# One PSUM bank per copy of transposed Q and K, and a new order of the work

## The chip, the core and the metric

The kernel runs on one core of one Trainium2 chip. The core has five engines with queues of their own: TensorE (PE in the profile; its weight loads are PEld), VectorE (DVE), ScalarE (ACT), GpSimd (POOL) and SyncE (SP), which here only issues transfers. Transfers between main memory and the core's SBUF run on 16 DMA engines. Matmul results land in PSUM, which has eight banks; here the whole of PSUM is one tile, `bank`, and the program names the bank of every step. The metric is device time in microseconds (us), median of the runs.

## The reference

For 8 batches and 8 heads, sequence 576, head size 64: causal attention with a decay, then a gated layer with a causal convolution of five taps.

```
scores = q @ k.T / 8
cum    = cumsum(max(s, 0))
scores = where(causal future, -1e9, scores + min(-(cum_i - cum_j), 0))
attn   = exp(scores - max) ; attn /= sum(attn)
x      = attn @ v                                # heads side by side: [8, 576, 512]
gate   = sigmoid(sum over k of conv_w[k] * x shifted by 4 - k)
out    = (gate * (x @ w_val)) @ w_out            # float32 [8, 576, 512]
```

The data are drawn once; q, k and v are float32 and are rounded to bfloat16 in the kernel.

## The kernel before, in words

The heads are worked in pairs: pair n = 4b + p holds heads 2p and 2p + 1 of batch b, 32 pairs in all. The steps of a pair, by the names that the program gives them:

- `ld_q`, `ld_k`, `ld_v`, `ld_t`, `ld_s` (L376 to L470) load. For batch 0, `ld_q.0.p` and `ld_k.0.p` bring the first 512 tokens of one pair. For later batches `ld_k.b` and `ld_q.b` each bring q and k together, `ld_q` for pairs 0 and 1, `ld_k` for pairs 2 and 3, into one of the tiles `first` or `qkf` (a slot number stands in the order). `ld_t` brings the last 64 tokens.
- `c_q`, `c_k` (L440) cast them to bfloat16 (`qkb`); `qt` (batch 0, L499) or `qq` (later batches, L647) transposes them on TensorE into PSUM; `qe` (L505) copies the transposed Q and K from PSUM into `QKT`. `tt` and `te` do the same for the last 64 tokens.
- `s0`, `s1`, `s2`, `s4` are the score matmuls, `e0`, `e1`, `e2`, `e4` the exponentials on ScalarE (L568, L544) and `mk` the causal mask on GpSimd (L591), for those pairs that are not masked by a matmul on TensorE (L530).
- `scan`, `decT`, `expw` make the decay weights from s, `vp` (L473) multiplies V by them on GpSimd, `av0` and `av` (L606) multiply the probabilities with that, `rec` and `nm` normalise, `xt` and `xe` transpose the result.
- `p2` to `p4` and `t1` to `t4` are the convolution on VectorE, GpSimd and ScalarE (L667, L678, L683, L686), `th` the tanh, `val` (L716) and `out` (L736) the two big products, `glu` the gating, `oe` and `st` the copy out and the store.
- `wu` (L632) multiplies the identity into a bank that nobody reads: work that only fills TensorE's time.

For batches 1 to 7 a step `qq.b.h` transposes pairs 2h and 2h + 1 and names two banks. Each pair takes sixteen transposes, eight for each of two token halves: r = 0 are the first 256 tokens, on 64 of the partitions, r = 1 the next 256, on the other 64. The half r goes into the r-th bank named, the first pair into its first 512 columns, the second into its last 512. A `qe.b.p` then copies pair p, and so reads one half of each of the two banks.

The order of all steps is written out in the string `ORDER` (L192), one entry per step: name, engine (S, G, T, A, V for SP, POOL, PE, ACT, DVE), PSUM banks or buffer slots. It comes from a planner. Each engine works off its own entries in that order. Waits between engines follow from the buffers that the steps read and write, and for PSUM from the banks. A transfer also waits until the one that used its completion counter eight transfers earlier has landed.

Of the kernel before, what the change touches and what calls it, by code (L numbers as in the profile page):

```python
# [212 lines left out]
te.2:A t1.4:V:3 av.5:T e1.7:A c_q.2:G:0 ld_v.3.2:S val.3.0:T:1 rec.5:V ld_t.4:S val.3.1:T:4 p4.4:A:0 nm.5:V
val.1.0:T:5 c_k.2:A:1 glu.3.0:V xt.5:T:6 t4.4:G glu.3.1:V ld_q.5:S:3 val.1.1:T:7 xe.5:V s2.7:T:3+4 glu.1.0:V
qq.2.0:T:1:2 t1.5:V:2 p2.5:G:1 e2.7:A val.0.0:T:5 glu.1.1:V glu.0.0:V qe.2.0:A val.0.1:T:7 t2.5:G t2.4:V av0.7:T:4+5
p3.5:A:0 av.7:T glu.0.1:V t3.4:V val.2.0:T:3 qe.2.1:A cast_wo:G qq.2.1:T:6:7 rec.7:V nm.7:V val.2.1:T:2 qe.2.3:A
xt.6:T:1 glu.2.1:V xt.7:T:0 t3.5:G qe.2.2:A glu.2.0:V s0.9:T:4+5:2 xe.6:V out.0.2:T:3 xe.7:V e0.9:A t1.6:V:1 p4.5:G:1
s1.9:T:6+7 t1.7:V:0 out.0.0:T:2 e1.9:A p3.6:G:0 t4.6:V s1.8:T:4+5 oe.0.2:A:0 s0.8:T:6+7:1 t4.7:V t4.5:G oe.0.0:A:1
val.7.0:T:3 e0.8:A t2.6:V st.0.0:S out.0.3:T:2 t2.7:V e1.8:A t3.6:G val.4.0:T:1 out.0.1:T:6 t3.7:V th.4:A:2 c_q.3:G:1
val.7.1:T:7 th.6:A:0 oe.0.3:V:2 val.4.1:T:0 glu.4.0:V th.7:A:1 oe.0.1:V:3 s2.8:T:4+5 s4.2.3:T:1+2 e2.8:A glu.4.1:V  # L220
st.0.1:S val.6.0:T:6 vp.2.0:G ld_v.3.3:S val.6.1:T:0 e4.2.3:A glu.6.0:V st.0.2:S glu.7.1:V s2.9:T:4+5 th.5:A:2
vp.2.1:G s0.10:T:1+2:0 ld_v.3.0:S glu.6.1:V av0.8:T:6+7 glu.7.0:V e2.9:A ld_v.3.1:S av.8:T vp.2.2:G val.5.0:T:3
st.0.3:S e0.10:A rec.8:V ld_q.4:S:1 nm.8:V s2.10:T:4+5 val.5.1:T:0 e2.10:A vp.2.3:G glu.5.0:V s1.10:T:6+7 glu.5.1:V
s0.11:T:1+2:1 ld_v.3.4:S e1.10:A xt.8:T:3 tt.3:T:0 ld_k.5:S:4 mk.10:G xe.8:V av0.9:T:4+5 e0.11:A t1.8:V:2 av.9:T
p4.8:G:0 qq.3.0:T:6:7 te.3:A rec.9:V nm.9:V s1.11:T:1+2 qe.3.0:A out.0.7:T:0 p3.8:G:1 t2.8:V qe.3.1:A av0.10:T:4+5
oe.0.7:V:1 c_k.3:G:1 xt.9:T:3 av.10:T e1.11:A xe.9:V s0.12:T:6+7:0 rec.10:V t1.9:V:0 out.0.6:T:0 e0.12:A mk.11:G
nm.10:V s1.12:T:1+2 oe.0.6:A:0 s2.11:T:6+7 t3.9:V xt.10:T:4 e1.12:A t3.8:G st.0.6:S out.0.8:T:0 ld_k.4:S:2 xe.10:V
e2.11:A t1.10:V:1 s2.12:T:1+2 c_q.5:G:0 tt.4:T:5 ld_v.4.1:S e2.12:A oe.0.8:V:3 qq.3.1:T:6:7 st.0.7:S t4.9:V qe.3.2:A
ld_v.4.0:S av0.11:T:1+2 t2.10:V p3.10:G:1 av.11:T ld_t.5:S qe.3.3:A out.0.4:T:0 rec.11:V t4.10:V t4.8:G te.4:A
st.0.8:S s0.14:T:6+7:1 nm.11:V out.0.5:T:4 e0.14:A oe.0.4:V:2 t3.10:G xt.11:T:5 th.8:A:2 t2.9:V s4.3.3:T:6+7 st.0.4:S  # L230
s0.13:T:0+1:2 ld_v.4.2:S e4.3.3:A xe.11:V mk.14:G s2.13:T:2+3 th.10:A:1 ld_v.4.4:S val.8.0:T:6 t1.11:V:2 val.10.0:T:7
e0.13:A ld_v.4.3:S vp.3.1:G glu.8.0:V t3.11:V ld_k.6:S:3 val.8.1:T:6 e2.13:A s1.13:T:0+1 glu.10.0:V c_q.4:G:1 t2.11:V
th.9:A:0 val.10.1:T:7 val.9.0:T:2 glu.8.1:V e1.13:A glu.10.1:V val.9.1:T:3 t4.11:V c_k.5:G:2 oe.0.5:A:0 s2.14:T:6+7
qq.5.0:T:0:1 e2.14:A glu.9.1:V st.0.5:S av0.13:T:4+5 qe.5.1:V av.13:T qe.5.0:A vp.3.2:G val.11.0:T:3 rec.13:V
glu.9.0:V th.11:A:1 s1.14:T:6+7 s0.15:T:0+1:2 nm.13:V val.11.1:T:2 vp.3.3:G e1.14:A glu.11.0:V xt.13:T:4 glu.11.1:V
e0.15:A s1.15:T:6+7 xe.13:V mk.12:G s2.15:T:2+3 out.1.1:T:5 t1.13:V:2 e1.15:A c_k.4:G:0 t2.13:V qq.5.1:T:0:1 e2.15:A
av0.14:T:6+7 qe.5.3:V av.14:T qe.5.2:A out.1.2:T:2 mk.15:G rec.14:V p4.13:A:1 nm.14:V qq.4.0:T:0:1 oe.1.1:A:3 t4.13:G
qq.4.1:T:6:7 oe.1.2:A:1 qe.4.1:V qe.4.0:A xt.14:T:5 out.1.0:T:2 vp.3.0:G t3.13:V xe.14:A av0.15:T:0+1 oe.1.0:A:2
t1.14:V:0 av.15:T p2.14:G:1 qe.4.2:A ld_v.5.4:S av0.12:T:2+3 rec.15:V ld_v.5.1:S av.12:T nm.15:V qe.4.3:A p4.14:G:0
tt.5:T:4 ld_v.5.2:S rec.12:V t3.14:V xt.15:T:0 te.5:A ld_v.5.0:S s0.16:T:6+7:0 xe.15:A nm.12:V s2.16:T:4+5 ld_v.5.3:S  # L240
vp.4.1:G e0.16:A t1.15:V:1 ld_t.6:S xt.12:T:3 s0.17:T:1+2:2 e2.16:A xe.12:V t2.14:G s4.4.3:T:6+7 t3.15:V ld_q.6:S:2
e0.17:A s1.16:T:4+5 t1.12:V:3 vp.4.0:G e4.4.3:A st.1.0:S t2.15:V val.14.0:T:1 st.1.1:S e1.16:A s1.17:T:6+7 t2.12:V
ld_k.7:S:4 t4.14:G val.14.1:T:2 e1.17:A t4.15:V av0.16:T:4+5 av.16:T ld_q.7:S:1 vp.4.3:G t4.12:V th.14:A:1 s2.17:T:6+7
out.1.3:T:0 rec.16:V e2.17:A t3.12:V st.1.2:S c_k.6:G:0 nm.16:V th.13:A:0 s0.18:T:6+7:0 val.12.0:T:3 e0.18:A
glu.14.1:V val.12.1:T:4 glu.14.0:V vp.4.2:G xt.16:T:2 oe.1.3:V:0 th.12:A:2 s4.5.3:T:6+7 xe.16:V s1.18:T:0+1 e4.5.3:A
glu.12.1:V val.13.0:T:5 mk.18:G e1.18:A glu.12.0:V s2.18:T:6+7 t1.16:V:3 val.13.1:T:3 vp.5.1:G e2.18:A glu.13.0:V
val.15.0:T:4 t4.16:V val.15.1:T:5 th.15:A:2 vp.5.2:G s0.19:T:6+7:1 glu.13.1:V av0.18:T:0+1 e0.19:A glu.15.1:V av.18:T
# [605 lines left out]
```

## Time and profile before

| what | us |
|---|---|
| median of 3 runs | 198.42 (197.47 to 199.06) |
| the profiled execution, its time | 198.85 |
| its span, first to last instruction | 197.0 |
| PE busy | 175.7 (89%) |
| ACT busy | 171.2 (87%) |
| POOL busy | 167.0 (85%) |
| DVE busy | 164.4 (83%) |

Durations in the profile come from the one profiled execution; its time lies 1.85 us above its span and 0.43 us above the median. In the rows, an arrow points from what is read to what is written (`out<-in`), the number after x is the count, and what stands behind "<-" in brackets is what ended the engine's idle time. L373 is the line of the helper that makes every plain copy, so its rows have to be told apart by the tile: `QKT<-bank` is a `qe` (or `te`), `qkb<-first` a cast.

### The profile page before, as it was taken

How to read it: one execution, taken by the hardware profiler on the slowest of the kernel's cores; microseconds unless marked ns; L12 is line 12 of the kernel's file. 1: busy time of each engine (PE TensorE's matmuls, PEld its weight loads, DVE VectorE, ACT ScalarE, POOL GpSimd, SP SyncE). 2: the span in 40 equal slices, each digit the busy share in tenths (PEclk: the TensorE clock that was granted, in tenths of full speed). 3: DMA queues.
4: the chain of work that ended last, by engine and by line, in shares of the span. 5: the costliest groups of instructions: out<-in, count | busy, mean ns of one | idle time of the engine just before them, and what ended most of it. 6: DMA issues, size and time to landing. Idle time of an engine off the chain costs nothing.

```text
span 197.0 us, 6662 instructions
## 1 busy us (share of the span) xinstructions
PE 175.7 (89%) x2716; PEld 115.6 (59%) x2716; DVE 164.4 (83%) x320; ACT 171.2 (87%) x229; POOL 167.0 (85%) x152
## 2 busy tenths in 40 slices
...
GB/s 169 280 202 207 239 259 253 276 254 284 279 145 287 271 323 297 319 339 236 292 88 225 236 405 330 211 204 255 8 208 61 3 0 161 112 3 106 5 174 205
DMA packets 62284, 40.46 MB, mean 205 GB/s; under 512 B 47334, under 2 KB 49382, under 8 KB 62251
## 3 DMA queue, kind: packets, MB, share of 16 engines
...
HBM read 30.57 MB, written 9.44 MB: 203 GB/s over the span
## 4 chain that ended last, share of the span: by engine, by line
PE 55%; ACT 19%; DVE 13%; DMA 6%; issue 3%; POOL 2%; ACTq 0%; DVEq 0%
PE bank L736 14%; ACT P L568 11%; PE bank L606 10%; PE bank L716 10%; PE bank L517 9%; DVE QKT L373 4%; DMA first<-in_q_dram 4%; ACT QKT L373 3%; PE bank L638 3%; DVE gp L683 3%; PE bank L641 3%; ACT th L703 3%; DVE glu L725 2%; PE bank L632 2%; DVE gp L678 2%
## 5 line engine op out<-in xcount | busy, mean ns | idle before, releaser
L568 ACT ACTIVATE P<-bank 128x1024 bf16<-128x1024 f32 x84 | 82.8, 1047 | 7.5 <-PE bank L517 5.1
L686 POOL TENSOR_TENSOR gp<-gp,pr 128x572 f32<-128x572 f32 (+6 forms) x37 | 46.1, 1250 | 7.1 <-DVE gp L683 3.6
L683 DVE SCALAR_TENSOR_TENSOR gp<-bank,cwr,gp 128x573 f32<-128x573 bf16 (+5 forms) x71 | 51.3, 743 | 0.5
L517 PE MATMUL bank<-QKT 64*128 64x128 bf16 (+4 forms) x592 | 39.6, 244 | 7.8 <-ACT P L568 3.5
L473 POOL TENSOR_TENSOR Vp<-vst,w 128x650 bf16<-128x650 f32 x32 | 40.5, 1283 | 0.8 <-ACT w L394 0.8
L716 PE MATMUL bank<-xT,wv 128*128 128x288 bf16 (+2 forms) x256 | 38.3, 286 | 1.1 <-ACT P L568 0.5
L606 PE MATMUL bank<-Vp,P 128*128 128x65 bf16 x960 | 36.4, 196 | 0.9 <-ACT QKT L373 0.4
L606 PEld LDWEIGHTS <-P 128*128 128x128 bf16 x960 | 33.6, 99 | 5.9 <-issue 2.9
L736 PE MATMUL bank<-wo,glu 128*128 128x512 bf16 x144 | 36.3, 380 | 0.0
L517 PEld LDWEIGHTS <-QKT 64*128 64x128 bf16 x592 | 20.4, 96 | 24.5 <-issue 19.7
L667 POOL TENSOR_TENSOR pr<-xT,cwr 128x572 f32<-128x572 bf16 (+6 forms) x28 | 27.5, 994 | 2.4 <-ACT xT L373 1.7
L725 DVE SCALAR_TENSOR_TENSOR glu<-th,bank 128x288 bf16<-128x288 f32 (+2 forms) x64 | 27.3, 446 | 2.3 <-PE bank L716 0.6
L716 PEld LDWEIGHTS <-wv 128*128 128x128 bf16 x256 | 22.6, 97 | 11.0 <-issue 4.8
L678 DVE SCALAR_TENSOR_TENSOR gp<-xT,cwr,bank 128x576 f32<-128x576 bf16 (+2 forms) x36 | 26.4, 741 | 2.0 <-ACT xT L373 1.2
L625 DVE TENSOR_TENSOR xn<-bank,recs 128x640 bf16<-128x640 f32 (+2 forms) x36 | 26.7, 744 | 0.6
L373 ACT COPY QKT<-bank 128x1024 bf16<-128x1024 bf16 (+1 forms) x24 | 23.0, 997 | 4.7 <-DVE QKT L373 2.0
L591 POOL TENSOR_SCALAR_AFFINE_SELECT P<-P 128x1024 bf16<-128x1024 bf16 (+2 forms) x22 | 23.1, 1052 | 4.0 <-ACT P L568 4.0
L703 ACT ACTIVATE th<-gp,cwr 128x576 f32<-128x576 f32 x28 | 21.9, 801 | 0.0
L736 PEld LDWEIGHTS <-glu 128*128 128x128 bf16 x144 | 12.3, 98 | 13.3 <-issue 2.3
L373 POOL CAST qkb<-first 128x512 bf16<-128x512 f32 (+2 forms) x11 | 12.0, 1095 | 7.2 <-DMA first<-in_q_dram 6.7
L373 ACT COPY ot<-bank 128x512 f32<-128x512 f32 x28 | 16.2, 605 | 2.0 <-PE bank L736 1.2
L373 DVE COPY QKT<-bank 128x512 bf16<-128x512 bf16 (+1 forms) x12 | 11.5, 956 | 7.1 <-PE bank L502 4.9
...
## 6 DMA issues: line engine op xcount, KB each, us to landing
out_dram<-ot SPq DMA_DIRECT2D x36, 256.0 KB, 3.2
vst<-in_v_dram SPq DMA_DIRECT2D x28, 256.0 KB, 5.4
...
vst<-in_v_dram SPq DMA_DIRECT2D x15, 128.0 KB, 5.1
first<-in_q_dram SPq DMA_DIRECT2D x6, 256.0 KB, 4.2
```

What stands on the lines that cost most here:

```text
L373: (act.copy if e is act else e.tensor_copy)(dst, src)
L473: e.tensor_tensor(Vps[b % 2][:, :, HP[p]], vslot(b)[:, :, HP[p]], w[:, :, b * 8 + 2 * p:b * 8 + 2 * p + 2].unsqueeze(3).to_broadcast([128, ...
L517: pe.matmul(ps[:, hh, c0:c0 + nq], QKTs[b % 2][r, 1, p, k0:k0 + 128], QKTs[b % 2][r, 0, p, q0:q0 + nq], **kw)
L568: act.activation(out=Pt(n)[:, :, step * 512:(step + 1) * 512], in_=pair((f"s{step}", n)), func=AF.Exp, scale=0.125)
L606: pe.matmul(ps[:, o:o + 65], lhsT, Vps[b % 2][:, kb, 2 * p + w, :], start=(kb == 0), stop=(kb == qb))
L678: vec.scalar_tensor_tensor(gp[:, lo:hi], xT[:, 3 + lo:3 + hi], r, xps(n, *h)[:, lo:hi], ALU.mult, ALU.add)
L683: vec.scalar_tensor_tensor(gp[:, lo:hi], xps(n, *h)[:, lo - m:hi - m], r, gp[:, lo:hi], ALU.mult, ALU.add)
L686: pool.tensor_tensor(gp[:, lo:hi], gp[:, lo:hi], prs[at[f"p{m}", n, *h][0]][:, lo:hi], ALU.add)
L703: act.activation(out=thof(n)[:, r], in_=gps[at["t1", n][0]].rearrange("p (h s) -> p h s", h=2)[:, r], func=AF.Tanh, scale=cwr[:, n % 4, 4:5])
L716: pe.matmul(ps, wv[:, dc, c * 128:(c + 1) * 128], xTs[b % 2][:, dc, 4 + lo:4 + hi], start=(dc == 0), stop=(dc == 3))
L725: vec.scalar_tensor_tensor(glu2[:, c, o + lo:o + hi], th[:, lo:hi], 1.0, ps, ALU.add, ALU.mult)
L736: pe.matmul(bank_of(u, i), glu2[:, c, i * 128:i * 128 + 128], wo[:, c, :], start=(c == 0), stop=(c == 3))
```

## The change

Three things change.

- A step `qe.b.p` of batches 1 to 7 no longer copies pair p. With h = p // 2 and r = p % 2 it copies token half r of both pairs 2h and 2h + 1, and so reads one whole bank and nothing of the other. The transposes write the same columns of the same banks as before.
- Of the loads of batch 0, ScalarE's queue issued `ld_k.0.0` to `ld_k.0.3`, `ld_q.0.2` and `ld_q.0.3`. Now it issues `ld_k.0.0` and `ld_k.0.1`, and SP issues the others.
- `ORDER` is planned anew: other places, banks and slots for most steps, and other engines for some. Batch 0's casts go to ScalarE (`c_q.0.0`, `c_k.0.2`) and VectorE (`c_k.0.1`, `c_q.0.2`) where GpSimd had them, and `c_q.0.3` the other way. There are 37 `wu` steps where there were 28. `s0.0` stands ahead of `tt.0`. The `ld_q`, `ld_k`, `ld_wo` of later batches use four slots where they used five.

The order's first lines, before and after, and the functions:

```diff
-ld_k.0.0:A ld_q.0.0:S ld_k.0.1:A wu.0:T:0 ld_t.0:S wu.1:T:7 wu.2:T:0 wu.3:T:7 ld_q.0.1:S wu.4:T:0 ld_k.0.2:A ld_s:S
-wu.5:T:7 ld_q.0.2:A wu.6:T:0 ld_v.0.0:S ld_k.0.3:A wu.7:T:7 c_k.0.0:V ld_q.0.3:A qt.0.0.k:T:0 wu.8:T:1 c_q.0.0:G
-qe.0.0.k:A wu.9:T:7 ld_v.0.1:S qt.0.0.q:T:1 c_k.0.1:G wu.10:T:0 qe.0.0.q:V wu.11:T:7 wu.12:T:0 wu.13:T:7 wu.14:T:2
-tt.0:T:0 ld_cw:S s0.0:T:1+2:0 te.0:V qt.0.1.k:T:3 c_q.0.1:G ld_v.0.2:S e0.0:A qe.0.1.k:V s1.0:T:4+5 s2.0:T:6+7
...
+ld_k.0.0:A ld_q.0.0:S ld_k.0.1:A wu.0:T:0 ld_t.0:S wu.1:T:7 wu.2:T:0 wu.3:T:7 ld_s:S wu.4:T:0 ld_k.0.2:S wu.5:T:7
+wu.6:T:0 ld_q.0.1:S wu.7:T:7 c_k.0.0:V ld_q.0.2:S qt.0.0.k:T:0 wu.8:T:1 c_q.0.0:A ld_v.0.0:S qe.0.0.k:V wu.9:T:7
+qt.0.0.q:T:1 c_k.0.1:V wu.10:T:2 wu.11:T:7 qe.0.0.q:V qt.0.1.k:T:0 wu.12:T:3 qe.0.1.k:A s0.0:T:1+2:0 ld_q.0.3:S
+tt.0:T:3 e0.0:A relu:V wu.13:T:7 ld_k.0.3:S wu.14:T:0 te.0:V wu.15:T:7 c_k.0.2:A wu.16:T:4 ld_v.0.1:S scan:V
...
+c_q.1.1:A rec.2:V s0.6:T:2+3:0 wu.32:T:7 nm.2:V wu.33:T:7 wu.34:T:7 t4.0:G e0.6:A nm.3:V s0.7:T:4+5:2 ld_t.2:S
...
+e4.1.3:A s1.5:T:2+3 t4.3:V th.1:A:1 wu.35:T:7 wu.36:T:7 vp.1.2:G th.2:A:2 av0.4:T:0+1 ld_q.3:S:3 av.4:T rec.4:V e0.5:A
...
 def qk_evac(e, b, p, *w):
...
         if ("qq", b, p // 2) in at:
-            copy(e, QKTs[b % 2][:, :, p, 0:512].rearrange("d w (r x j) -> d w r x j", r=2, j=8),
-                 both_rows(b, p).rearrange("d r (j x w) -> d w r x j", w=2, j=8))
+            h, r = divmod(p, 2)
+            copy(e, QKTs[b % 2][:, :, 2 * h:2 * h + 2, r * 256:r * 256 + 256].rearrange("d w p (x j) -> d p w x j", j=8),
+                 row_bank(b, h, r).rearrange("d (p j x w) -> d p w x j", p=2, w=2, j=8))
             return
...
-    def both_rows(b, p):
-        lo, hi = sorted(at["qq", b, p // 2])
-        return bank16[:, lo:hi + 1:hi - lo, p % 2 * 512:p % 2 * 512 + 512]
+    def row_bank(b, h, r):
+        return bank16[:, at["qq", b, h][r], :]
 
     def qk_T2(e, b, h):
         for p in range(2):
             for j in range(8):
                 for r in range(2):
-                    half_T(both_rows(b, 2 * h + p)[:, r, j * 64:j * 64 + 64], qk_src(None, b, 2 * h + p, j), r)
+                    half_T(row_bank(b, h, r)[:, p * 512 + j * 64:p * 512 + j * 64 + 64], qk_src(None, b, 2 * h + p, j), r)
```

More of the change, by code (lines that the diff above doesn't have):

```diff
@@ L213 @@
[L213 to L247, printed above, removed]
@@ new lines @@
+glu.6.0:V ld_q.4:S:3 glu.7.1:V s0.10:T:0+1:0 th.5:A:2 c_k.3:G:0 s2.9:T:6+7 glu.6.1:V av0.8:T:3+4 glu.7.0:V e2.9:A
+av.8:T st.0.2:S val.5.0:T:2 e0.10:A rec.8:V nm.8:V s2.10:T:6+7 vp.2.1:G val.5.1:T:5 e2.10:A glu.5.0:V st.0.3:S
+s1.10:T:3+4 glu.5.1:V s0.11:T:0+1:1 vp.2.2:G e1.10:A xt.8:T:2 av0.9:T:6+7 xe.8:V av.9:T ld_v.3.4:S e0.11:A t1.8:V:3
+p4.8:G:1 tt.3:T:3 ld_v.3.3:S qq.3.0:T:4:5 rec.9:V te.3:A nm.9:V mk.10:G ld_v.3.1:S s1.11:T:0+1 qe.3.1:A out.0.7:T:3
+t2.8:V st.0.1:S p3.8:G:0 qe.3.0:A av0.10:T:6+7 oe.0.7:V:1 xt.9:T:2 av.10:T e1.11:A vp.2.3:G xe.9:V ld_v.3.0:S
@@ new lines @@
+t1.15:V:0 xt.12:T:0 s0.17:T:6+7:2 t2.14:G e2.16:A xe.12:V ld_q.6:S:2 s4.4.3:T:2+3 t3.15:V e0.17:A s1.16:T:4+5
+t1.12:V:2 vp.4.0:G e4.4.3:A t2.15:V val.14.0:T:6 e1.16:A t4.14:G s1.17:T:2+3 t2.12:V val.14.1:T:7 st.1.2:S e1.17:A
+t4.15:V av0.16:T:4+5 av.16:T vp.4.2:G t4.12:V th.14:A:0 s2.17:T:2+3 ld_t.6:S out.1.3:T:1 rec.16:V e2.17:A t3.12:V
+vp.4.1:G nm.16:V th.13:A:1 s0.18:T:2+3:0 ld_k.7:S:3 val.12.0:T:0 c_k.6:G:0 e0.18:A glu.14.1:V val.12.1:T:4 oe.1.3:V:3
+xt.16:T:7 th.12:A:2 glu.14.0:V s4.5.3:T:1+2 xe.16:V s1.18:T:5+6 e4.5.3:A glu.12.1:V mk.18:G val.13.0:T:3 e1.18:A
@@ new lines @@
+t3.18:V ld_v.6.3:S av0.19:T:1+2 c_k.7:G:1 th.16:A:2 ld_t.7:S oe.1.6:V:1 s2.20:T:5+6 xt.17:T:0 e2.20:A t4.18:V av.19:T
+out.1.5:T:7 xe.17:V qe.6.1:A t2.18:G rec.19:V t1.17:V:2 s0.21:T:5+6:1 ld_v.6.4:S oe.1.5:A:0 s1.20:T:3+4 nm.19:V
+c_q.7:G:0 out.1.8:T:7 e1.20:A st.1.6:S t2.17:V ld_v.6.2:S xt.19:T:1 e0.21:A out.1.7:T:4 t3.17:V vp.5.0:G oe.1.8:A:2
+xe.19:V s2.21:T:5+6 st.1.3:S s1.21:T:2+3 t4.17:V e2.21:A val.16.0:T:7 p3.19:G:0 t1.19:V:3 val.16.1:T:0 e1.21:A
+ld_v.7.0:S val.17.0:T:5 glu.16.0:V p4.19:G:1 glu.16.1:V val.18.0:T:6 th.17:A:1 t2.19:V s0.22:T:2+3:2 ld_v.7.4:S
@@ new lines @@
+qq.7.0:T:0:7 e0.22:A glu.17.0:V t3.19:G val.18.1:T:1 ld_v.7.3:S qe.7.0:V val.17.1:T:5 th.18:A:2 av0.21:T:2+3 mk.22:G
+oe.1.7:A:1 glu.18.1:V av.21:T qe.7.1:A glu.17.1:V st.1.7:S s0.23:T:0+1:1 glu.18.0:V st.1.5:S t4.19:G s2.22:T:4+5
+rec.21:V e0.23:A ld_v.7.1:S av0.20:T:6+7 nm.21:V av.20:T e2.22:A ld_v.7.2:S vp.6.0:G s4.6.3:T:0+1 rec.20:V xt.21:T:2
+nm.20:V st.1.8:S val.19.0:T:3 th.19:A:2 vp.6.2:G s1.22:T:4+5 e4.6.3:A glu.19.0:V val.19.1:T:6 e1.22:A xe.21:V
+xt.20:T:3 glu.19.1:V vp.6.3:G s1.23:T:0+1 xe.20:V p3.21:A:1 s2.23:T:6+7 out.2.1:T:4 t1.20:V:3 e1.23:A vp.6.1:G
@@ new lines @@
+t1.21:V:0 out.2.2:T:5 e2.23:A t3.20:V p4.21:G:0 qq.7.1:T:0:1 oe.2.2:A:0 t2.21:V av0.22:T:6+7 qe.7.3:A av.22:T t2.20:V
+t3.21:G out.2.3:T:2 oe.2.1:A:1 rec.22:V t4.20:V qe.7.2:A st.2.1:S tt.7:T:1 t4.21:G nm.22:V s0.26:T:4+5:2 th.20:A:2
+out.2.0:T:0 te.7:V e0.26:A oe.2.3:V:2 vp.7.1:G xt.22:T:3 oe.2.0:A:1 s2.26:T:6+7 xe.22:V s0.24:T:4+5:0 e2.26:A
+av0.23:T:1+2 st.2.0:S t1.22:V:3 p2.22:G:0 st.2.2:S av.23:T e0.24:A st.2.3:S s0.25:T:6+7:1 rec.23:V p4.22:G:1 nm.23:V
+e0.25:A s1.24:T:4+5 t3.22:V xt.23:T:2 vp.7.0:G e1.24:A s2.24:T:0+1 xe.23:V s1.25:T:6+7 val.20.0:T:3 t1.23:V:2
@@ new lines @@
+nm.24:V t4.25:G xe.26:A av0.27:T:4+5 glu.23.1:V p3.25:A:0 xt.24:T:1 t1.26:V:2 av.27:T xe.24:A out.2.8:T:7 t3.25:G
+glu.23.0:V p4.26:A:1 t1.24:V:0 out.2.5:T:0 oe.2.8:A:2 rec.27:V t4.26:G t2.24:V th.25:A:1 st.2.8:S u0.28:T:2+3:1
+nm.27:V out.2.6:T:7 f0.28:A p4.24:G:0 t3.24:V oe.2.5:A:0 xt.27:T:4 u0.29:T:2+3:0 oe.2.6:A:1 st.2.5:S chk0:V
+u1.28:T:0+1 xe.27:A out.2.4:T:5 f1.28:A t1.27:V:3 t4.24:G val.25.0:T:7 f0.29:A val.24.0:T:0 t2.26:V oe.2.4:A:0
+out.2.7:T:1 p2.27:G:1 t3.27:V th.24:A:2 st.2.4:S u1.29:T:5+6 st.2.6:S glu.25.0:V oe.2.7:A:2 u0.30:T:2+3:1 p3.26:G:0
```

128 lines of the change are left out of this document (66 added, 62 removed).

## The prediction

> **What bounds the kernel now.** I read the page's head first (busy us, share, instructions), then the engines by stage, then the waits.
>
> ```profile
> PE 175.7 (89%) x2716; PEld 115.6 (59%) x2716; DVE 164.4 (83%) x320; ACT 171.2 (87%) x229; POOL 167.0 (85%) x152
> ...
> 0.00:10.00 10.00, 6.31 (x29) 2.60 (x31) 3.43 (x13) 1.87 (x2) 3.86 (x14) 1.00 0.82 227
> 10.00:20.00 10.00, 7.21 (x64) 4.04 (x64) 6.14 (x9) 7.01 (x9) 7.18 (x7) 0.57 0.97 204
> 30.00:40.00 10.00, 6.46 (x123) 4.17 (x124) 8.92 (x14) 9.30 (x12) 8.77 (x7) 0.93 0.98 261
> 60.00:80.00 20.00, 19.89 (x338) 13.35 (x333) 18.16 (x33) 19.91 (x26) 19.57 (x15) 1.00 1.05 293
> 80.00:100.00 20.00, 17.83 (x319) 11.60 (x316) 17.74 (x30) 17.92 (x24) 17.77 (x14) 1.00 0.99 291
> 160.00:180.00 20.00, 19.41 (x263) 12.48 (x260) 18.93 (x45) 19.12 (x32) 18.18 (x18) 1.00 0.19 68
> ```
>
> The columns of the stages are length, busy PE, PEld, DVE, ACT, POOL, granted clock, DMA share and GB/s. No engine is the bound by itself: four of them are at 83 to 89% over the whole span. From 60 to 80 us PE and ACT have 0.1 us to spare out of 20, and from 160 to 180 PE has 0.6. So what a change can win lies where the engines stand: in the first 40 us, where PE is idle 3.5 us between 30 and 40 and its clock falls to 0.57 between 10 and 20, and between 80 and 100, where PE and ACT both lose some 2 us against the stage before. Transfers are busy nearly throughout the first 100 us (0.82 to 1.05), so bytes cannot come much faster; only their order can change.
>
> **The copies of Q and K.** The hole at 80 to 100 is made by the copies that the change cuts anew:
>
> ```profile
> ACT QKT L373 <- DVE QKT L373: 2.0, 3, 0.8
> DVE QKT L373 <- ACT QKT L373: 0.9, 1, 0.9
> ...
> 88.55 1.23 DVE L373 COPY QKT<-bank 128x1024 bf16<-128x1024 bf16 x1
> 89.81 1.01 ACT L373 COPY QKT<-bank 128x1024 bf16<-128x1024 bf16 x1 [0.72 <-DVE QKT L373]
> 90.87 0.59 PE L517 MATMUL bank<-QKT 64*128 64x448 bf16 x10 [0.79 <-ACT QKT L373]
> 94.73 1.23 DVE L373 COPY QKT<-bank 128x1024 bf16<-128x1024 bf16 x1
> 95.99 1.01 ACT L373 COPY QKT<-bank 128x1024 bf16<-128x1024 bf16 x1 [0.84 <-DVE QKT L373]
> 97.05 1.11 PE L641 MATMUL bank<-ident,qkb 64*128 64x64 bf16 x64 [0.55 <-ACT QKT L373]
> 99.06 1.01 ACT L373 COPY QKT<-bank 128x1024 bf16<-128x1024 bf16 x1 [0.46 <-DVE QKT L373]
> ...
> 28.93 1.01 ACT L373 COPY QKT<-bank 128x1024 bf16<-128x1024 bf16 x1 [0.68 <-PE bank L641]
> 29.97 1.23 DVE L373 COPY QKT<-bank 128x1024 bf16<-128x1024 bf16 x1
> ```
>
> The first number of a row is its start, the second its length. Where the two copies of a set go to different engines, the second starts 0.03 us after the first has ended (88.55 + 1.23 = 89.78, then 89.81), though both were ready together: each reads a half of both banks, so a wait keeps them apart. There are six such sets, by the names of their `qq`: 1.0, 1.1, 4.0, 5.0, 5.1 and 7.0; the rows at 88.55, 94.73 and 99.06 belong to 5.0, 5.1 and 4.0. After the change the two copies touch different banks, and in the new program's list of waits the second copy of 5.0, 4.0, 7.0 and of both sets of batch 1 waits for PE alone (those of 5.1 still list the other engine too, for a reason that the list doesn't tell). What goes is the idle time in brackets: 0.72 + 0.84 + 0.46 = 2.0 us on ACT, and 0.79 + 0.55 = 1.3 us on PE, between 89 and 100. Next in line there is ACT's own work, which is full at 0.1 us in 20 when nothing holds it, so a gain of PE's 1.3 to ACT's 2.0 us should hold. I take **-1.7 us**. For the sets outside that stage (the two of batch 1, and one of batch 7), the waits list has 0.9 us of DVE idle; PE's 3.5 idle us at 30 to 40 have other causes too, so I take **-0.3 us**. Bounds of both together: 0 and -3.
>
> The new copies' form is not in the trace. Their nearest rows are the old ones:
>
> ```profile
> L373 ACT COPY QKT<-bank x24: 585/1018/1117, 5.9 to 143.4; 128x1024 bf16<-128x1024 bf16 x22, 128x512 bf16<-128x512 bf16 x2
> L373 DVE COPY QKT<-bank x12: 673/958/1225, 6.3 to 133.8; 128x512 bf16<-128x512 bf16 x6, 128x1024 bf16<-128x1024 bf16 x6
> ```
>
> Twice a copy of 512 elements would be 1.17 us on ACT and 1.35 on DVE, against 1.02 and 1.23 now. So 28 copies at the same price, 0, is what I take; at +0.12 each on the path of one engine in three it would be +1.1, and a shorter one would give as much.
>
> A copy now brings half of two pairs, so a pair's scores wait for both copies. Where one engine makes both (eight sets), the first pair's scores become ready 1.02 us later. The new order puts the scores of those sets behind other pairs' scores, which cover that: **0**, and with the cover gone 1.0 us on one or two sets.
>
> **The start.** The first exponential, and the second pair:
>
> ```profile
> 0.81 1.55 ACTq L430 DMA_DIRECT2D first<-in_k_dram  x3
> 4.56 0.39 SPq L430 DMA_DIRECT2D first<-in_q_dram  x1
> 4.57 0.60 DVE L373 CAST qkb<-first 128x512 bf16<-128x512 f32 x1 [1.16 <-DMA first<-in_k_dram]
> 4.65 1.28 ACT L373 ACT_TABLE_LOAD   x1 [4.65 <-DMA first<-in_q_dram]
> 6.32 0.69 DVE L373 COPY QKT<-bank 128x512 bf16<-128x512 bf16 x1 [1.15 <-PE bank L502]
> 9.38 0.63 PE L481 MATMUL bank<-identf,tail 128*128 128x128 f32 x4 [1.56 <-DMA tail<-in_k_dram]
> 10.38 1.94 ACT L568 ACTIVATE P<-bank 128x1024 bf16<-128x1024 f32 x2 [3.85 <-PE bank L517]
> 11.99 1.47 POOL L373 CAST qkb<-first 128x512 bf16<-128x512 f32 x2 [5.93 <-DMA first<-in_q_dram]
> ...
> first<-in_k_dram ACTq DMA_DIRECT2D x4, 256.0 KB, 4.8
> tail<-in_q_dram SPq DMA_DIRECT2D x8, 128.0 KB, 6.4
> gp<-in_s_dram SPq DMA_DIRECT2D x1, 144.0 KB, 7.1
> ```
>
> Pair 0's Q and K are copied by 6.32 + 0.69 = 7.0, but its scores stand behind the tail's transposes in PE's queue, which wait for a transfer until 9.38. In the new order `s0.0` is ahead of `tt.0`. VectorE then casts k of pair 0 (to 5.17), copies K (to some 6.3), casts k of pair 1 (0.41 to 0.61) and copies Q (0.69): done near 7.5, so the first exponential starts at about 8.0 in place of 10.38, **2.4 us earlier**.
>
> The second pair's q was issued at 4.56 and used at 11.99: ScalarE's loads of later pairs were under way ahead of it and shared the bandwidth. In the new order only s, the tails and one k are ahead of it on SP, and it is issued without the wait to 4.56. The bytes up to its end are then 5 loads of 256 KB, its own among them, two tails of 128 KB and s with 144 KB, 1.7 MB; at 227 GB/s that is 7.5 us, and with the 0.81 us before the first issue it lands near 8.5, some 3 us earlier.
>
> The Trainium skill (DMA: Bandwidth & Descriptors, "Issuing engines are not separate DMA queues") speaks against this part: issuing from several engines only saves the issuing sequencer's time, and the loads share the same DMA engines whoever issues them. By it nothing lands sooner on the whole, and four more issues on SP cost their issue times. The rows agree as to the sum of bytes (share 0.97 from 10 to 20); by the skill's rule alone the start would be worth 0, or a loss; that is the second rival.
>
> How much of 2.4 is kept? The next fixed point is batch 1's V, which the same transfers bring:
>
> ```profile
> L470 SPq DMA_DIRECT2D vst<-in_v_dram x2: 866/2718/4570, 29.0 to 33.6; - x2
> DMA to landing us min/median/max: 6.2/7.3/8.5
> 41.07 3.76 POOL L473 TENSOR_TENSOR Vp<-vst,w 128x650 bf16<-128x650 f32 x3
> 42.24 1.44 PE L632 MATMUL bank<-ident 128*128 128x512 bf16 x3
> 43.47 2.71 PE L606 MATMUL bank<-Vp,P 128*128 128x65 bf16 x54
> 45.37 1.02 ACT L568 ACTIVATE P<-bank 128x1024 bf16<-128x1024 f32 x1 [1.37 <-PE bank L606]
> ```
>
> The last of these loads lands 6.2 us after 33.6, at 39.8; the order of bytes up to it is about the same in the new order, so `vp.1.0` can move from 41.07 to 39.8 and no further. That keeps 1.3 us. Behind it stand 1.44 us of fillers, some 1.2 of them after `vp.1.0` has ended (41.07 + 3.76/3 = 42.3), until the `av` at 43.5; the new order has two fillers there in place of three. I take **-1.3 us**; bounds 0 and -2.4.
>
> **Fillers and moved steps.**
>
> ```profile
> L632 PE MATMUL bank<-ident x28: 376/512/634, 1.4 to 43.0; 128*128 128x512 bf16 x28
> 30.00:40.00 10.00, 0.39 (x1) 0.10 (x1) 0.93 0.98 261
> sum 60.00, PE 10.37 PEld 2.97; mean PE 1.48 PEld 0.42
> ```
>
> The two lower rows are of the stages again, for the fillers alone. Nine more fillers are 9 x 0.38 to 9 x 0.51, 3.4 to 4.6 us of PE. Most stand where PE is idle (3.5 us from 30 to 40, against one filler there now, and 2.8 from 10 to 20), and a busier PE may hold its clock there. A filler delays what stands behind it where the plan's times are off: before `av` above, 1.2 us of the 10.37 that all fillers take did so, an eighth. An eighth of 4.6 is **+0.6**, which I take; bounds -0.5 (clock) and +4.6.
>
> On the engines, two casts come to ScalarE (0.60 us each as on VectorE above) and three leave GpSimd; ScalarE loses an `oe` and two conv products net and gets two `xe`. These are under 1 us per engine, in stages that have it: **0**, bounds -1 and +1.
>
> The sum: -1.7 - 0.3 - 1.3 + 0.6 = **-2.7 us**. Against the profiled execution's own 198.85 (span 197.0 and 1.85 around it) that is 196.1; the median of the runs lies 0.43 lower, so the forecast is 198.42 - 2.7 = **195.7 us**.
>
> **Rivals.** (1) All of it comes: the start keeps 2.4, the copies give 3.0, the fillers cost nothing: -5.4, **193.0**. For it: every wait above is real idle time. Against: 160 to 180 shows an almost full PE, and V of batch 1 holds the start. (2) The start gives nothing, since bytes arrive as before, and the copies give 1.7 with fillers at +0.6: -1.1, **197.3**. For it: the DMA share. The same time band holds the case that the change does not do what it says: other waits keep copies apart, as they might in 5.1, and nothing else is won: -0.5 to 0, about **198**. (3) Slower: the fillers lie on the path. Seven of them (28 to 34) stand around the scores of pairs 6 and 7; if PE reaches them at half clock while ScalarE has already finished what they are meant to span, each holds up a score product by 0.51 us and the exponential behind it, and the whole plan behind that: 9 x 0.51 = 4.6, less 1.7 for the copies, +2.9, **201.3**. It decides where the wait after those fillers is ScalarE's for PE: above 5 fillers on the path the gain of copies and start is used up (5 x 0.51 = 2.6 of 2.7). For it: the row at 45.37, where ScalarE waited 1.37 us behind fillers; a new order of 1160 steps can make such holes anywhere. Against: PE's idle time at 30 to 40.
>
> **How the numbers follow.** A measurement of this kernel tells about 1% from no change (the runs shown spread by 0.8%). Chances: the forecast's case 0.50 (194.2 to 197.2), rival 1 0.10, rival 2 and its like 0.21 (196.6 to 199.6), rival 3 0.19 (199.6 to 203). Faster than 196.4 are seven tenths of the first case, rival 1 and little of the second: 0.47. Slower than 200.4 are nine tenths of the third and nothing else: 0.18. The rest, 0.35, is within 1%. The range leaves out half of the slower case and a bit of rival 1: 192.8 to 201.2.
>
> **What would show it.** After the change: the two entries of ACT and DVE waiting for each other's QKT copies are gone from the waits, and in the mixed sets the two copies overlap; PE and ACT between 80 and 100 are at 19 or more of 20. The first exponential starts at 8.0 (7.5 to 9), the second pair's q is cast at 8.5 to 9.5; `vp.1.0` starts at 39.8 to 41. A copy costs 1.0 on ACT and 1.2 on DVE. Wrong would make it: copies at 1.2 and 1.35, fillers ahead of idle ScalarE between 33 and 45, or a load that ScalarE or GpSimd waits for after 20 us.

## The result and the profile after

| | before | after |
|---|---|---|
| median of 4 runs, us | 198.59 (197.47 to 199.06) | 191.47 (191.0 to 193.65) |
| ratio after to before | | 0.967 [0.960, 0.974] |
| the profiled execution, its span | 197.0 | 191.6 |

The change makes the kernel faster by 7.1 us. The forecast was 2.7 us, and the time lies 1.3 us below the lower end of its range. The profiled execution of after is its slowest run, 193.65 us, 2.2 us above the median. Medians are of all runs (one of 320.12 us stands among the four of the experiment that moves all stores), while ratios and their intervals leave out runs more than 1.5% above the fastest of their kernel.

The stages of after, in the columns of those of before (length, busy PE, PEld, DVE, ACT, POOL, granted clock, DMA share, GB/s), below the busy times of the whole span:

```profile
PE 175.1 (91%) x2725; PEld 115.4 (60%) x2725; DVE 164.3 (86%) x321; ACT 171.4 (89%) x230; POOL 164.4 (86%) x149
...
0.00:10.00 10.00, 8.34 (x45) 3.81 (x45) 5.64 (x18) 3.94 (x5) 3.14 (x13) 1.00 0.87 218
10.00:20.00 10.00, 9.02 (x150) 6.08 (x146) 6.77 (x10) 8.89 (x14) 8.67 (x9) 1.00 1.05 240
30.00:40.00 10.00, 6.72 (x87) 4.14 (x87) 7.67 (x11) 8.42 (x11) 8.74 (x8) 0.73 0.95 231
60.00:80.00 20.00, 17.97 (x317) 11.49 (x315) 15.56 (x29) 17.88 (x22) 18.30 (x15) 1.00 1.12 271
80.00:100.00 20.00, 18.62 (x372) 13.38 (x371) 18.22 (x32) 19.16 (x27) 18.19 (x14) 1.00 1.08 269
160.00:180.00 20.00, 19.80 (x266) 13.06 (x261) 19.04 (x48) 19.04 (x32) 17.88 (x23) 1.00 0.23 82
```

The work is nearly the same (PE 175.1 for 175.7, ACT 171.4 for 171.2); idle time has gone. The first 20 us hold more of it: ACT has done 12.8 us of work by 20 us (3.94 + 8.89), where before it had done 8.9. From 80 to 100 PE and ACT gain 0.8 and 1.2 us. From 60 to 80, PE loses 1.9 us against before; a later run suggests that this belongs to this one execution.

Where the lead arises can be seen from one group of instructions that both kernels have 84 times, the wide exponentials of ScalarE (82.8 us in all before, 82.6 after). The table gives the time at which a given share of their total is done in before, and how much earlier each other kernel is there. The times come from windows of half a microsecond of one profiled execution each, so they are good to some tenths, and the shares are rounded (12% is an eighth). The other rows are experiments below.

| share done | 1% | 6% | 12% | 25% | 38% | 44% | 56% | 62% | all |
|---|---|---|---|---|---|---|---|---|---|
| before, at us | 11.2 | 19.2 | 25.7 | 47.6 | 69.3 | 77.2 | 94.9 | 109.2 | 159.9 |
| after, lead in us | 1.9 | 3.3 | 4.1 | 5.1 | 5.2 | 3.1 | 2.3 | 4.6 | 5.0 |
| before, copies by bank | 0.1 | 0.7 | 0.1 | 1.0 | 1.0 | 1.0 | 1.8 | 3.4 | 4.0 |
| before, four loads by SP | 1.3 | 3.7 | 3.4 | 3.5 | 3.6 | 3.6 | 3.7 | 2.6 | 3.0 |
| after, four loads by ScalarE | 2.1 | 0.6 | 1.4 | 3.3 | 3.4 | 2.4 | 1.7 | 4.0 | 4.4 |
| after, tail ahead of first scores | 1.4 | 2.9 | 3.7 | 4.2 | 4.3 | 4.3 | 4.3 | 6.7 | 7.0 |
| after, copies by pair | 2.0 | 3.5 | 4.4 | 3.3 | 0.0 | 0.0 | -3.0 | -6.6 | -13.5 |

After wins 4 us by 26 us and 5 by 48, loses nearly 3 between 69 and 95 in this execution, and wins 2.3 between 95 and 109. The first number of a row of its timeline is the start, the second the length:

```profile
4.42 0.62 ACT L374 CAST qkb<-first 128x512 bf16<-128x512 f32 x1 [1.26 <-DMA first<-in_q_dram]
8.51 1.02 ACT L570 ACTIVATE P<-bank 128x1024 bf16<-128x1024 f32 x1
9.49 0.61 POOL L374 CAST qkb<-first 128x512 bf16<-128x512 f32 x1 [5.97 <-DMA first<-in_q_dram]
10.98 0.63 SPq L436 DMA_DIRECT2D first<-in_q_dram  x1
36.72 3.76 POOL L474 TENSOR_TENSOR Vp<-vst,w 128x650 bf16<-128x650 f32 x3 [0.37 <-DMA vst<-in_v_dram]
...
85.59 1.22 DVE L374 COPY QKT<-bank 128x1024 bf16<-128x1024 bf16 x1
86.07 1.01 ACT L374 COPY QKT<-bank 128x1024 bf16<-128x1024 bf16 x1
91.18 1.01 ACT L374 COPY QKT<-bank 128x1024 bf16<-128x1024 bf16 x1 [0.69 <-PE bank L643]
91.29 1.22 DVE L374 COPY QKT<-bank 128x1024 bf16<-128x1024 bf16 x1 [1.13 <-PE bank L643]
94.61 1.23 DVE L374 COPY QKT<-bank 128x1024 bf16<-128x1024 bf16 x1 [0.39 <-PE bank L643]
94.84 1.03 ACT L374 COPY QKT<-bank 128x1024 bf16<-128x1024 bf16 x1
```

The first exponential starts at 8.51 (before 10.38), the second pair's q is cast at 9.49 (11.99), and `vp.1.0` starts at 36.72 (41.07). The two copies of a set now lie over each other: 85.59 to 86.81 on DVE and 86.07 to 87.08 on ACT. What they wait for is PE's transposes, no longer each other, and their durations are those of before.

### The profile page after: what moved, and what is told of

The parts are those of the page before. It is cut to its first block, busy times and chain, and to the rows that moved or that the text cites. A ratio compares the mean times of both kernels' runs of the same rounds, so it can differ in the third digit from the quotient of the medians.

```text
span 191.6 us, 6672 instructions
## 1 busy us (share of the span) xinstructions
PE 175.1 (91%) x2725; PEld 115.4 (60%) x2725; DVE 164.3 (86%) x321; ACT 171.4 (89%) x230; POOL 164.4 (86%) x149
## 4 chain that ended last, share of the span: by engine, by line
PE 37%; ACT 27%; POOL 9%; DVE 8%; DMA 8%; issue 7%; SPq 0%; ACTq 0%; POOLq 0%; DVEq 0%
ACT P L570 17%; PE bank L737 9%; PE bank L608 8%; DMA out_dram<-ot 6%; PE bank L519 5%; PE bank L717 5%; ACT th L704 5%; POOL gp L687 3%; PE bank L634 3%; PE bank L640 2%; POOL pr L668 2%; DMA first<-in_k_dram 2%; POOL qkb L374 2%; ACT ot L374 2%; DVE xn L627 2%
## 5 line engine op out<-in xcount | busy, mean ns | idle before, releaser
L570 ACT ACTIVATE P<-bank 128x1024 bf16<-128x1024 f32 x84 | 82.6, 1047 | 4.8 <-PE bank L608 1.8
L684 DVE SCALAR_TENSOR_TENSOR gp<-bank,cwr,gp 128x572 f32<-128x572 bf16 (+4 forms) x72 | 51.9, 741 | 0.4 <-ACT pr L666 0.2
L687 POOL TENSOR_TENSOR gp<-gp,pr 128x572 f32<-128x572 f32 (+6 forms) x36 | 45.0, 1256 | 8.3 <-DVE gp L684 4.6
L519 PE MATMUL bank<-QKT 64*128 64x128 bf16 (+4 forms) x592 | 38.2, 239 | 5.5 <-ACT P L570 4.0
L608 PE MATMUL bank<-Vp,P 128*128 128x65 bf16 x960 | 37.2, 197 | 0.3 <-ACT P L570 0.3
L608 PEld LDWEIGHTS <-P 128*128 128x128 bf16 x960 | 34.2, 100 | 5.0 <-issue 2.0
L519 PEld LDWEIGHTS <-QKT 64*128 64x128 bf16 x592 | 19.4, 94 | 23.4 <-issue 17.9
L668 POOL TENSOR_TENSOR pr<-xT,cwr 128x572 f32<-128x572 bf16 (+6 forms) x29 | 28.7, 997 | 0.9 <-DVE xT L374 0.6
L593 POOL TENSOR_SCALAR_AFFINE_SELECT P<-P 128x1024 bf16<-128x1024 bf16 (+1 forms) x22 | 22.4, 1019 | 2.1 <-ACT P L570 1.9
L374 POOL CAST qkb<-first 128x2048 bf16<-128x2048 f32 (+2 forms) x10 | 13.4, 1337 | 6.5 <-DMA first<-in_q_dram 6.1
L640 PE MATMUL bank<-ident,xn 128*128 128x128 bf16 x164 | 15.0, 220 | 1.5 <-DVE gp L684 0.8
```

The lines of the kernel that those rows point to most:

```text
L374: (act.copy if e is act else e.tensor_copy)(dst, src)
L519: pe.matmul(ps[:, hh, c0:c0 + nq], QKTs[b % 2][r, 1, p, k0:k0 + 128], QKTs[b % 2][r, 0, p, q0:q0 + nq], **kw)
L570: act.activation(out=Pt(n)[:, :, step * 512:(step + 1) * 512], in_=pair((f"s{step}", n)), func=AF.Exp, scale=0.125)
L608: pe.matmul(ps[:, o:o + 65], lhsT, Vps[b % 2][:, kb, 2 * p + w, :], start=(kb == 0), stop=(kb == qb))
L668: pool.tensor_tensor(pr, xTs[b % 2][:, c, 4 + lo - m:4 + hi - m], r.to_broadcast([128, hi - lo]), ALU.mult)
L684: vec.scalar_tensor_tensor(gp[:, lo:hi], xps(n, *h)[:, lo - m:hi - m], r, gp[:, lo:hi], ALU.mult, ALU.add)
```

## The experiments

The first theory is that of the prediction. The rivals: the start gives much more and the rest little; the new order with its fillers and their clock makes the gain; the copies make it. The part of a diff in capitals and colons is an edit of `ORDER`.

**The new order with the old copies.** Copies by pair again, as before the change. The second copies of two sets (`qe.2.1`, `qe.6.1`) stand a few places earlier, ahead of steps that write one of the set's own banks, since no bank of a set is free now before both copies are done.

```diff
-            h, r = divmod(p, 2)
-            copy(e, QKTs[b % 2][:, :, 2 * h:2 * h + 2, r * 256:r * 256 + 256].rearrange("d w p (x j) -> d p w x j", j=8),
-                 row_bank(b, h, r).rearrange("d (p j x w) -> d p w x j", p=2, w=2, j=8))
+            copy(e, QKTs[b % 2][:, :, p, 0:512].rearrange("d w (r x j) -> d w r x j", r=2, j=8),
+                 both_rows(b, p).rearrange("d r (j x w) -> d w r x j", w=2, j=8))
...
```

> The changed kernel with the old copies (a copy takes pair p from halves of both banks) and its new order of work; two copies are moved up in program order so that no bank is written between them. Start theory (the gain was made by batch 0's loads, casts and order, before 45 us; the copies give some 2 us between 86 and 105): 193 to 194, the waits of ACT and DVE for each other's QKT copies are back, and the lead over the kernel before is still 5 us at 60 us. Copy theory (the copies made most of the 7 us): 196 to 198.

Measured: 211.78 us, ratio to before 1.071 [1.067, 1.075], 20 us slower than after. No theory had that. The lead of the start is there (4.4 us at 12%), and is lost from then on, up to -13.5. Two of its waits, and rows of its timeline:

```profile
ACT QKT L372 <- DVE QKT L372: 5.3, 4, 2.1
PE bank L637 <- ACT QKT L372: 4.9, 4, 2.4
```

```profile
24.78 1.01 ACT L372 COPY QKT<-bank 128x1024 bf16<-128x1024 bf16 x1 [0.21 <-PE bank L605]
...
25.84 1.53 PE L605 MATMUL bank<-Vp,P 128*128 128x65 bf16 x45 [1.10 <-ACT QKT L372]
...
101.49 1.01 ACT L372 COPY QKT<-bank 128x1024 bf16<-128x1024 bf16 x1 [1.31 <-DVE QKT L372]
102.56 0.69 PE L637 MATMUL bank<-ident,xn 128*128 128x128 bf16 x5 [2.43 <-ACT QKT L372]
```

Other engines, and PE above all, wait for these copies, though they work in other banks. The row at 25.84 is `av.2` in banks 4 and 5; the copy from 24.78 reads banks 3 and 7. The row at 102.56 is `xt.14`, which writes bank 5; the copy from 101.49 reads banks 7 and 2. In both, the step that waits works in a bank that lies between the two named by the copy. The planner of before gave every `qq` two neighbouring banks. The new order has 3 and 7, 3 and 6, 7 and 4, 0 and 4, 0 and 7, 3 and 0, 7 and 2 among its pairs. So this is not the price of the copies alone; a run that names one bank per copy was needed:

**The new order, pair by pair, each copy cut in two.** A pair's copy becomes two of half the size, one for each bank; the same two copies as in the run above stand earlier.

```diff
-            h, r = divmod(p, 2)
-            copy(e, QKTs[b % 2][:, :, 2 * h:2 * h + 2, r * 256:r * 256 + 256].rearrange("d w p (x j) -> d p w x j", j=8),
-                 row_bank(b, h, r).rearrange("d (p j x w) -> d p w x j", p=2, w=2, j=8))
+            for r in range(2):
+                copy(e, QKTs[b % 2][:, :, p, r * 256:r * 256 + 256].rearrange("d w (x j) -> d w x j", j=8),
+                     row_bank(b, p // 2, r)[:, p % 2 * 512:p % 2 * 512 + 512].rearrange("d (j x w) -> d w x j", w=2, j=8))
```

> The changed kernel with each copy of pair p made as two copies of half the size, one from each bank (28 more instructions, by 2 x 0.58 against 1.02 us some 3 us more on ScalarE). The copies of a set share banks as with the old copies, but no instruction names two banks. If the kernel with the old copies lost 20 us because a copy from two banks that aren't neighbours holds the banks between them too: 193 to 197. If it lost them because the two copies of a set wait for each other and free both banks late: 204 and more.

Measured: 195.99 us, ratio 0.989 [0.982, 0.996]. Of the 20 us lost, 16 are back, with the same pairs sharing the same banks; what differs is that no copy names two banks. Together with the rows above this shows where they went: a copy that names two banks apart holds the banks between them in this program. The other 4.5 us above after were not taken apart: there are twice as many copies, two of 605 ns (median) against one of 1.02 us, and some still share a bank (ACT waits 1.1 us for DVE's copies, in two places).

```profile
L372 ACT COPY QKT<-bank x46: 585/605/703, 7.2 to 140.2; 128x512 bf16<-128x512 bf16 x46
```

**The old order with the new copies.** The change's `qk_evac`, `row_bank` and `qk_T2` in the kernel before, its `ORDER` untouched.

> The kernel before with the new copies alone, its order of work kept. Start theory: 196 to 197.5, the stage 80 to 100 gets its 2 us back and nothing comes before 60 us. Copy theory: 192 to 194.

Measured: 195.13 us against 198.02, ratio 0.987 [0.980, 0.995]: the copies alone give 2.9 us, by the interval 1.0 to 4.0. The two entries of ACT and DVE waiting for each other are gone from its waits, and the stage from 80 to 100 has no hole (before: PE 17.83, ACT 17.92):

```profile
80.00:100.00 20.00, 19.28 (x388) 14.01 (x391) 19.28 (x34) 19.96 (x29) 19.60 (x16) 1.00 1.00 286
```

In the table its lead is 1.0 us from 25% on, behind the two sets of batch 1; it grows by 2.4 between 77 and 109 us, where those of batches 4 and 5 lie; and by 0.6 after that. This is one execution, and its 4.0 us in all are more than the 2.9 of the medians.

**After with the old issuers.** ScalarE issues the four loads again.

```diff
-ld_k.0.2:S ... ld_q.0.2:S ... ld_q.0.3:S ... ld_k.0.3:S
+ld_s:S ld_k.0.2:A ld_q.0.2:A ld_k.0.3:A ld_q.0.3:A
```

> The changed kernel with four of batch 0's loads (k and q of pairs 2 and 3) issued by ScalarE again, as before. Start theory with the loads as its main part: the second pair's q is cast at 11 to 12 in place of 9.5, and 193 to 195 us. If only the order on PE and the casts count, not who issues: 191 to 192.

Measured: 193.69 us, ratio 0.980 [0.974, 0.986], 2.2 us above after; the two intervals just touch. The second pair's q is late again, as in before:

```profile
12.01 0.61 POOL L372 CAST qkb<-first 128x512 bf16<-128x512 f32 x1 [8.48 <-DMA first<-in_q_dram]
```

**Before with the loads of after**, in their order and from their engines, nothing else changed:

```diff
-... ld_q.0.1:S ld_k.0.2:A ld_s:S ld_q.0.2:A ld_v.0.0:S ld_k.0.3:A c_k.0.0:V ld_q.0.3:A
+... ld_s:S ld_k.0.2:S ld_q.0.1:S ld_q.0.2:S ld_v.0.0:S ld_q.0.3:S c_k.0.0:V ld_k.0.3:S
```

> The kernel before with batch 0's loads issued as in the changed kernel (SP issues four more, s and the second pair's q earlier); nothing else. Load theory (worth 2 us, as its undoing cost 2.2): 196 to 197, the second pair's q cast near 9.5. If the new loads only pay with the new order behind them: 197.5 to 198.5.

Measured: 196.00 us against 197.79, ratio 0.991 [0.988, 0.995]. Its lead is 3.4 us at 6% and still 3.5 at the end: in the profiled execution all of it is kept. `vp.1.0` moves by as much, to 37.77:

```profile
9.39 1.18 POOL L372 CAST qkb<-first 128x512 bf16<-128x512 f32 x2 [3.22 <-DMA first<-in_q_dram]
37.77 3.76 POOL L472 TENSOR_TENSOR Vp<-vst,w 128x650 bf16<-128x650 f32 x3
```

**Before, the four loads issued by SP in the old order**, to tell the issuer from the order:

```diff
-ld_k.0.2:A ... ld_q.0.2:A ... ld_k.0.3:A ... ld_q.0.3:A
+ld_k.0.2:S ... ld_q.0.2:S ... ld_k.0.3:S ... ld_q.0.3:S
```

> The kernel before with the same four loads of batch 0 issued by SP, but in the old order of the program (the second pair's q ahead of them, s behind the first of them). If it counts that the later pairs' loads no longer run beside the second pair's q (who issues): the second pair's q is cast at 9 to 10, and 196 to 196.5 as with the new order of loads. If the new order of loads counts (s early, q of the second pair without a wait for a landing): 197.5 to 199.

Measured: 196.46 us against 199.29 (10 runs), ratio 0.986 [0.981, 0.991]. Four letters give 2.8 us (1.8 to 3.8 by the interval); the new order of the loads adds nothing that shows. Two things go. In before SP itself waited 1.8 us for a load of ScalarE's to land ahead of the second pair's q (first fence, from SP's own waits), and this load was then under way together with ScalarE's. Here it is issued at 2.75 for 4.56, and used at 7.71 for 11.99 (second fence): 5.0 us later, where it took 7.4.

```profile
SPq L430 <- DMA first<-in_k_dram: 1.8, 1, 1.8
```

```profile
2.75 0.62 SPq L429 DMA_DIRECT2D first<-in_q_dram  x1
...
7.71 0.61 POOL L372 CAST qkb<-first 128x512 bf16<-128x512 f32 x1 [1.59 <-DMA first<-in_q_dram]
```

That it is used at 7.71 here and at 9.39 in the run before, with the same lead (3.7 and 3.4 us at 6%), suggests that below 9.4 something else sets the start. What that is was not separated; the tail and s land earlier in both runs too (the tail at 7.0 and 7.1 for 9.2, s at 9.5 and 8.1 for 12.5).

**Before with loads, copies, and the first scores ahead of the tail.**

```diff
-tt.0:T:0 ld_cw:S s0.0:T:1+2:0
+ld_cw:S s0.0:T:1+2:0 tt.0:T:0
```

together with the loads of after (the run two above) and the new copies.

> The kernel before with the new loads, the new copies and s0.0 ahead of tt.0, its order else kept. If the three named parts make the gain: 192 to 194 (2.9 of the copies, 2 of the loads, 0.5 to 1 of the first scores). If the new plan as a whole is needed: 195 and more.

Measured: 192.40 us against 197.79, ratio 0.971 [0.966, 0.976]: 5.4 of the 7.1 us without the new plan. The rest, some 1 to 2 us, lies within the intervals of the two ratios (after: 0.960 to 0.974), so whether the new plan gives anything more is open.

**After with the first scores behind the tail again.**

```diff
-qe.0.1.k:A s0.0:T:1+2:0 ld_q.0.3:S tt.0:T:3
+qe.0.1.k:A tt.0:T:3 s0.0:T:1+2:0 ld_q.0.3:S
```

> The changed kernel with tt.0 ahead of s0.0 again, as before. If the first scores' place is part of the start's gain: the first exponential 0.5 to 1 us later, 192 to 192.8 us. If the second pair's load alone sets the start: 191.5 us, though the first exponential is later.

Measured: 191.44 us (191.26 to 191.77), ratio 0.967 [0.960, 0.974], that of after. The place of the first scores is worth nothing that the runs can tell. Its profiled execution (191.37) is a typical one, and has a lead of 7.0 us at the end, without the loss after 69 us that the one of after shows.

**After with batch 0's casts on their old engines.**

```diff
-c_q.0.0:A ... c_k.0.1:V ... c_k.0.2:A ... c_q.0.2:V ... c_q.0.3:G
+c_q.0.0:G ... c_k.0.1:G ... c_k.0.2:G ... c_q.0.2:G ... c_q.0.3:V
```

> The changed kernel with batch 0's casts on the engines of before (GpSimd has six of them in place of three). If moving the casts off GpSimd is part of the start's gain: 192.5 to 194, the start of the weighted V (vp.0.0) 1 to 2 us later. If the casts are covered: 191.5.

Measured: 192.37 us (190.53 to 192.71), ratio 0.969 [0.963, 0.976], not to be told from after.

**After without 27 of its 37 fillers**, `wu.10` to `wu.36`:

> The changed kernel without its fillers from the eleventh on (27 of 37). Clock theory (the fillers hold PE's clock at 1.0 from 10 to 30 us, where it was 0.57 and 0.92 before, and that made the start): the clock falls to 0.6 from 10 to 20, and 193.5 to 196 us. If the fillers only cost, as the prediction charged them: 190 to 191.5.

Measured: 191.99 us, ratio 0.975 [0.966, 0.983]. The clock does fall, to 0.66 in this stage, where after has 1.00:

```profile
10.00:20.00 10.00, 7.74 (x106) 5.71 (x106) 4.97 (x10) 8.19 (x12) 8.15 (x9) 0.66 1.08 256
```

and yet no time is lost that the runs could tell. So the clock did not make the gain. The intervals of the two ratios overlap, and a cost or a gain of the fillers of some 2 us could hide in them.

**The loss between 64 and 83 us.** In the profiled execution of after two engines wait there for stores, which stand behind loads of batches 3 and 4 in SP's queue:

```profile
69.36 0.69 DVE L374 COPY ot<-bank 128x512 f32<-128x512 f32 x1 [1.34 <-DMA out_dram<-ot]
72.76 0.58 ACT L374 COPY ot<-bank 128x512 f32<-128x512 f32 x1 [1.14 <-DMA out_dram<-ot]
```

Three stores were put ahead of the loads:

```diff
-st.0.0:S ... ld_q.4:S:3 ... st.0.2:S ... st.0.3:S ... st.0.1:S
+st.0.0:S st.0.2:S st.0.3:S st.0.1:S ... ld_q.4:S:3
```

> The changed kernel with three stores of the first output rows (st.0.2, st.0.3, st.0.1) moved in SP's queue ahead of the load of batch 4's q and of batch 3's V. If the 2 to 3 us that the changed kernel loses between 64 and 83 us come from stores that stand behind those loads (copies out wait for the buffer, 1.1 and 1.3 us): the waits on out_dram go, and 189 to 190.5 us. If they come from the load of the engines there: 191 to 192.

Measured: 192.37 us, ratio 0.970 [0.965, 0.975]: no gain. The stage from 60 to 80 is full again, and the next one loses it; there two copies of ACT wait 1.9 us for stores:

```profile
60.00:80.00 20.00, 19.54 (x336) 12.71 (x338) 17.67 (x33) 19.93 (x26) 19.45 (x16) 1.00 1.08 251
80.00:100.00 20.00, 17.55 (x370) 12.86 (x371) 17.27 (x30) 18.01 (x25) 18.07 (x14) 1.00 1.07 287
```

With every store of the first three groups right behind the copy that fills it:

> The changed kernel with every store of the first three groups of output rows right behind its copy out in the order. If late stores cost the copies out some 2.5 us in all between 64 and 100 and nothing takes their place: 189 to 190.5. If the loads behind them then come late, or the loss moves as it did with three stores: 191 to 193.

Measured: 193.59 us, ratio 0.977 [0.966, 0.988], no gain either, though in its profiled execution (191.73) no copy waits for a store between 60 and 100. The kernel with the tail first has the same order of stores as after, and its lead is 4.3 us at 38, 44 and 56% alike. So the loss most likely belongs to the profiled execution of after, which lies 2.2 us above its median, and there is little to win from it in a usual run; why that execution has it stays open.

## Why the prediction was right and wrong

**The bound.** That no engine is the bound, and that the gain lies in the first 40 us and at 80 to 100, holds in the main. The sentence "bytes cannot come much faster; only their order can change" does not: it read the DMA share as a limit. From 10 to 20 us before moves 204 GB/s at 0.97, after 240 at 1.05. The Trainium skill (Perfetto Trace Analysis, "Identifying the Most-Contended Engine") says that occupancy misleads for DMA, since there are 16 engines, and that throughput should be read instead; these two rows agree, with 18% more GB/s at a share 8% higher. As the two stages hold different transfers, a better sign is the last V of batch 1: the same loads stand ahead of it in both orders, and it lands at 36.6 where it landed at 39.8.

**The copies.** The mechanism was right as put: the mutual waits are gone, the copies overlap, a copy costs what it cost. The term was -2.0 for a measured -2.9, near its bound of -3; the measured interval, 1.0 to 4.0 us, holds both. By the leads of single executions, -1.7 at 80 to 100 was too small, where the lead shows 2.4, more than the 2.0 of ACT's idle time that was taken as the upper end; and so was -0.3 elsewhere, where the lead shows 1.0 (batch 1) and 0.6 (the end). The 0.9 us of DVE in the waits list is not spread over these sets, as the prediction has it, but stands before one copy of batch 7, at 133.83:

```profile
133.83 1.23 DVE L373 COPY QKT<-bank 128x1024 bf16<-128x1024 bf16 x1 [0.93 <-ACT QKT L373]
```

The copies of batch 1 are kept apart too (28.93 and 29.97 in the prediction's rows), but DVE had other work until just before, so the list names nothing for them. PE at 19 or more between 80 and 100 was reached with the copies alone (19.28), not in after's profiled execution (18.62). The zero for a copy that brings half of two pairs, and the equal price of the new form, hold. That copies of one bank let the planner choose two banks apart without holding those between was not seen.

**The start.** Two landmarks came as said: the first exponential at 8.51 (7.5 to 9), the q at 9.49 (8.5 to 9.5). The step that failed is "the order of bytes up to it is about the same in the new order, so `vp.1.0` can move from 41.07 to 39.8 and no further". The loads ahead are indeed the same, but `vp.1.0` started at 36.72, 3.1 us below that floor, since V itself came sooner. Its last load in after:

```profile
L471 SPq DMA_DIRECT2D vst<-in_v_dram x1: 2502/2502/2502, 31.0 to 31.0; - x1
DMA to landing us min/median/max: 5.6/5.6/5.6
```

31.0 + 5.6 is 36.6, where before it landed at 39.8. The landing was no fixed point: SP issues in order, and its issues wait for earlier landings. Ahead of batch 1's first load SP spent 5.5 us in such waits in before (1.8, 1.8, 0.9, 0.6, 0.4) and 1.6 in after, with fifteen issues of its own ahead in both. The difference, 3.9 us, is what that load gained: it went out at 10.98; before, at

```profile
14.91 0.63 SPq L435 DMA_DIRECT2D first<-in_q_dram  x1
```

So an earlier start brings the next loads forward with it. Measured, the loads alone give 1.8 and 2.8 us by the medians of the two runs (1.1 to 2.5 and 1.8 to 3.8 by the intervals), against the 1.3 taken. The 2.4 us that bounded this term were read from the first exponential and put down to `s0.0` ahead of `tt.0`, which gives nothing that shows. What gives the gain is the loads that land sooner; the second pair's q is one, the tail and s are others, and which of them counts was not separated.

**Rival 2**, with the Trainium skill's rule that a second issuing engine only saves issue time (DMA: Bandwidth & Descriptors, "Issuing engines are not separate DMA queues"), had the start at nothing. The run with four letters changed decides against that use of the rule: who issues is worth 2.8 us here, and it goes the other way, one issuer being better than two. The same page ("Queues, rings and completion order") has each DMA engine take turns between queues packet by packet. The packets in the traces show both queues in the same microseconds, but no even turns: from 7 to 9 us of before, ScalarE's queue moved 0.53 MB and SP's 0.03, though the second pair's q had been issued on SP at 4.56. With the four letters changed, SP's moved 0.54 MB in these 2 us and ScalarE's none. That fits the 7.4 us for the load that ran beside ScalarE's and 5.0 without them; why the turns were so uneven stays open.

**Fillers** at +0.6: measured near 0 (191.99 without, 191.47 with), and the runs can't tell +0.6 from nothing. **Rival 3**, fillers on the path, falls with it. **Casts and moved steps** at 0: for the casts no run shows otherwise (192.37 with the old ones); for the moved steps it stays open. **Rival 1**, "all of it comes", 193.0, was nearest, and it too lay above the result. Copies (2.9) and loads (1.8 to 2.8) make 4.7 to 5.7 of the 7.1 us; whether the rest is the new plan or lies in the spread of the runs stays open.
